# A 4 KB descriptor ring, five unread products on TensorE, and chunk 2's Am written by masked operations

## The chip, the core and the metric

The kernel runs on one core of a Trainium2 chip. The metric is the device time of one execution, in microseconds (us); three executions of the kernel before took 699.11, 699.98 and 702.73 us, so the median is 699.98 us. One more execution was recorded by the profiler and took 696.41 us; all rows below come from that one.

## What is computed

A linear recurrence over 768 steps for 4 x 8 heads of width 40, whose output of 3072 rows of 320 goes through a mixture of eight experts, one expert for each row.

```python
for t in range(S):                       # attention, per batch and head, state is 40 x 40
    y[t]  = r[t] @ state
    Sa    = state @ a[t]
    state = state * w[t] - outer(Sa, b[t]) + outer(v[t], k[t])
x = y.transpose(0, 2, 1, 3).reshape(3072, 320)
e = argmax(x @ w_gate, axis=1)           # one expert of 8 for each row
out = prob[e] * sigmoid(x @ w_output_gate)[e] * (relu(x @ w1[e]) @ w2[e])
```

## The kernel before

The 768 steps are cut into 12 chunks of 64. For each chunk c there are four kinds of work.

- `scan(c)` loads w and D (the a, k and b of the chunk, 1080 KB) and forms running products P and I of the decays on VectorE (DVE in the rows).
- `prep(c)` forms Av (a times decays; on VectorE for chunks 0 and 1, on GpSimd, POOL in the rows, from chunk 2 on) and KBt (k and b times decays, on VectorE), and spreads Av over a block matrix Am: of 120 partitions, three groups of 40 hold three groups of heads, and each head's columns are zero outside its own group. The product KBt x Am (tile `pl`, L213) then gives the chunk's coupling matrices, which ScalarE (ACT) copies into N and LA (L224, L226) and GpSimd masks (L228). Transposes (`back`, tile `pt`, L155) turn KBt into KB and Wp into WT.
- `tinv` inverts the triangular matrices of N on VectorE, alone for chunks 0 and 1 and in pairs after that; its result is copied to Tc by ScalarE (L319) for chunks 0 and 1.
- `crit(c, q)` and `tail(c, q)` carry the state through the chunk for each half q of the batches: products `pa` (L365, L378), with steps As on ScalarE (L369) and, for chunks 0 and 1, on VectorE (L391), then `pS`, `pM` and `pY`.

`run` interleaves these generators. The final order on each engine is made when the program is built, by a scheduler that places what it holds ready first; `issue_after` pins a block behind a given instruction of the same engine. Engines take their instructions in that order, each waiting for its semaphores, so an instruction that waits holds back all that stand behind it on its engine.

In `prep`, chunk 0 writes Am with three masked operations (one on ScalarE, two on VectorE, each with a mask `hj` over one group of partitions as scale). All later chunks fill only the non-zero blocks by three transfers on SyncE's queue (L184), and copy Av into LA by three more (`strips`, L170). `Am`, `KBt`, `Av`, `D`, `P` and `I` have one buffer each. Tiles `pl` and `pt` share two PSUM buffers. `warm` runs 40 unread products before the first input is there.

After the attention, `experts` gathers token rows with indirect transfers issued by GpSimd (L800), multiplies (L831, L844 to L846) and scatters rows (L849). GpSimd also scatters the routing table (`tab`, L712). GpSimd's transfers use descriptors kept in a ring in SBUF.

Of the kernel before, what the change touches and what calls it, by code (L numbers as in the profile page):

```python
# [9 lines left out]
F32 = mybir.dt.float32  # L10
F32R = mybir.dt.float32r
BF16 = mybir.dt.bfloat16
# [37 lines left out]
def pat(x, off, dims):  # L50

    return bass.AP(x.tensor, x.offset + off, [x.ap[0]] + [list(d) for d in dims])


class Att:
    npool = 0

    def __init__(s, ctx, tc, ident, stage, win, din, rl, vl, vt, nch=12):
        s.stage = stage
        s.tc, s.nc, s.nch, s.ident = tc, tc.nc, nch, ident  # L60
        s.win, s.din, s.rl, s.vl, s.vt = win, din, rl, vl, vt
        nc = s.nc
        pool = lambda n, b, **k: ctx.enter_context(tc.tile_pool(name=n, bufs=b, **k))
        s.p5, s.p2, s.cp = (pool(f"p{i}", i) for i in (5, 2, 1))
        s.ps = pool("ps", 1, space=PSUM)
        s.dr = pool("dr", 2, space=DRAM)
        s.pre = ExitStack()
        s.p1 = s.pre.enter_context(tc.tile_pool(name="p0", bufs=1))
        s.mM = s.cp.tile([128, C], F32, name="mM")
        nc.gpsimd.memset(s.mM, 1.0)  # L70
        for h in range(2):
            nc.gpsimd.affine_select(out=s.mM[64 * h:64 * h + 64], in_=s.mM[64 * h:64 * h + 64], pattern=[[1, C]],
                                    base=0, channel_multiplier=-1, compare_op=ALU.is_gt, fill=0.0)

        s.Am = s.p1.tile([120, 2, NP, 66], F32, name="Am")
        s.rst = s.p1.tile([120, 792], BF16, name="rst")
        with tc.high_priority():
            nc.vector.memset(s.rst, 0.0)
            nc.vector.memset(s.rst[:, 0:792:33], 1.0)
        s.Tt = s.p1.tile([128, 1056], F32, name="Tt")  # L80
        nc.gpsimd.memset(s.Tt, 0.0)
        nc.gpsimd.memset(s.Tt[:, 0:1056:33], 1.0)


        s.hj = s.cp.tile([120, 3], F32, name="hj")
        nc.vector.tensor_reduce(out=s.hj, in_=s.ident[0:120, 0:120].rearrange("p (j s) -> p j s", j=3), axis=AX.X, op=ALU.add)
        s.hm = s.cp.tile([128, 2], F32, name="hm")
        nc.vector.tensor_reduce(out=s.hm, in_=s.ident.rearrange("p (x h s) -> p h x s", x=4, h=2), axis=AX.XY, op=ALU.add)
        s.hq = s.cp.tile([128, 2], F32, name="hq")
        nc.vector.tensor_reduce(out=s.hq, in_=s.ident.rearrange("p (x h s) -> p h x s", x=2, h=2), axis=AX.XY, op=ALU.add)  # L90
        s.wb = s.cp.tile([120, 1], F32, name="wb")
        nc.gpsimd.memset(s.wb, -0.9)
        s.wsq = s.cp.tile([120, nch], F32, name="wsq")
        s.rqm = s.cp.tile([120, nch], F32, name="rqm")
        s.zb = s.cp.tile([128, 32], F32, name="zb")
        nc.gpsimd.memset(s.zb, 0.0)
        s.buffers()
        s.st, s.ld, s.post, s.idle, s.mark = {}, {}, [], False, {}
# [25 lines left out]
    def warm(s, src, n):  # L124
        fl = s.ps.tile([128, 512], F32, name="fl", tag="pS")
        for _ in range(n):
            s.nc.tensor.matmul(fl[0:32, 0:src.free_size()], s.zb[0:src.partition_size()], src, start=True, stop=True)

    def prep(s, c):

        nc = s.nc
        g, V = nc.gpsimd, nc.vector
# [18 lines left out]
        def back(dst, src):  # L151
            for g0, n, nj in ((0, 4, 3), (4, 2, 2)):
                pt = s.ps.tile([128, n, 40 * nj], F32, name="pt", tag="pl", bufs=2)
                for i in range(n):
                    nc.tensor.transpose(out=pt[:, i], in_=src[0:40 * nj, g0 + i].rearrange("p n t -> p (n t)"),  # L155
                                        identity=s.ident[0:40 * nj, 0:40 * nj])
                nc.scalar.copy(out=pat(dst, 40 * g0, [(240, nj), (40, n), (1, 40)]),
                                     in_=pt.rearrange("p g (j e) -> p j g e", j=nj))
                yield
# [7 lines left out]
        def strips():  # L167
            for j in range(3):
                ng = 6 if j < 2 else 4
                nc.sync.dma_start(out=LA[0:40, :, 6 * j:6 * j + ng, :], in_=Ag[40 * j:40 * j + 40, :, 0:ng])  # L170
# [7 lines left out]
        with s.tc.issue_after(s.mark['n', 0]) if c == 1 else ExitStack():  # L178
            nc.scalar.copy(out=Av[:, :, 64:66], in_=P[:, :, :, 32])
        Ag = Av.rearrange("p (a g) t -> p a g t", a=2)  # L180
        if c:
            for j in range(3):
                r, n = slice(40 * j, 40 * j + 40), 6 if j < 2 else 4
                am = nc.sync.dma_start(out=s.Am[r, :, 6 * j:6 * j + n], in_=Ag[r, :, 0:n]).ins  # L184
                s.mark['am', c] = am
            with s.tc.issue_after(am):
                strips()
        else:
            for j, (e, n) in enumerate(((nc.scalar, 6), (V, 6), (V, 4))):
                o, i, m = s.Am[:, :, 6 * j:6 * j + n, 0:64], Ag[:, :, 0:n, 0:64], s.hj[:, j:j + 1]  # L190
                if e is nc.scalar:
                    e.activation(out=o, in_=i, func=AF.Copy, scale=m)
                else:
                    e.tensor_scalar(out=o, in0=i, scalar1=m, scalar2=None, op0=ALU.mult)
            s.later = strips
        yield
        KBt = s.p1.tile([120, 12, 2, C], F32, name="KBt")
        with s.tc.issue_after(s.mark['r', 0]) if c == 1 else ExitStack():
# [7 lines left out]
        for side in range(2):  # L206
            Am = s.Am[:, side]
            yield
            for g0 in range(0, 6, 2):
                pl = s.ps.tile([128, 2, 3, C], F32, name="pl", tag="pl" if c or g0 == 0 else "tl", bufs=2 if c or g0 == 0 else 3)  # L210
                nj = 3 if g0 < 4 else 2
                for i in range(2):
                    nc.tensor.matmul(pl[:, i, 0:nj], KBt[:, 6 * side + g0 + i].rearrange("p n t -> p (n t)"), Am[:, g0 + i:g0 + i + 6 * nj - 5:6, 0:64],  # L213
                                     start=True, stop=True)
                pv = pl.rearrange("p g j t -> p j g t")
                for h in range(2):
                    r = slice(64 * side + 32 * h, 64 * side + 32 * h + 32)
                    n = C - 32 * h
# [12 lines left out]
        split()  # L231
        for side in range(2):
            yield from back(KB[:, side], KBt[:, 6 * side:6 * side + 6])
        yield from back(WT, Wp)
        yield

# [333 lines left out]
class Moe:  # L570
# [324 lines left out]
    def experts(s, ctx, verdict):  # L895
# [21 lines left out]
        def unit(e, t0, nt, prep):  # L917

            for _ in s.expert(nt, W[e], T[e, t0], lambda: s.hp, ps1, ps2) if (e, t0) != (0, 0) else s.E0:
                next(prep, None)  # L920
            for _ in prep:
                pass
# [197 lines left out]
```

## Time and profile before

| what | value |
|---|---|
| time, median of 3 (lowest to highest) | 699.98 us (699.11 to 702.73) |
| profiled execution, its own time | 696.41 us |
| its span, first to last instruction | 694.7 us |
| PE (TensorE) busy | 635.5 us, 91% |
| DVE (VectorE) busy | 463.8 us, 67% |
| ACT (ScalarE) busy | 338.2 us, 49% |
| POOL (GpSimd) busy | 229.7 us, 33% |
| mean granted clock of TensorE | 0.959 |

The span starts with the first instruction; 1.7 us of the execution lie around it. A busy PE is not a PE at its peak, and the granted clock stands at one of two levels, 1.00 or 0.50 of 2.4 GHz. In the rows, a time in brackets is how long the engine had been idle and, after the arrow, what ended that.

### The profile page before, as it was taken

The numbers are of one execution on the slowest core, as the hardware profiler recorded it, in microseconds if no ns is written. First come the engines' busy times: TensorE is split into PE (matmuls) and PEld (weight loads), VectorE is DVE, ScalarE is ACT, GpSimd is POOL, SyncE is SP. The second block draws the span as 40 slices with busy tenths as digits, with TensorE's granted clock in tenths as the row PEclk, the third lists the DMA queues.
The fourth block names the chain that finished last, engine by engine and source line by source line (L and its number), as shares of the span: only waits on it lengthen the run. The fifth ranks groups of instructions, "written<-read, shape, count | busy, mean of one in ns | idle before, by whom it ended". The sixth has DMA issues, their size and how long they took to land.

```text
span 694.7 us, 21145 instructions
## 1 busy us (share of the span) xinstructions
PE 635.5 (91%) x8866; PEld 568.2 (82%) x8866; DVE 463.8 (67%) x911; ACT 338.2 (49%) x782; POOL 229.7 (33%) x334
## 2 busy tenths in 40 slices
PE   7596987899999999999999899889999999999993
PEld 7375776788988888888898798789989989898993
DVE  8858689969987995998499544633774555444230
ACT  2576763774477367538733443432653444334110
POOL 9643321441343366224223102355241243311111
PEclk9657999999999999999999999999999999999997
DMA  5995662276356527633235822442673353510000
GB/s 139 174 187 135 173 154 69 86 175 163 103 144 162 126 84 192 162 95 103 63 81 171 232 69 71 137 124 74 202 218 110 102 176 113 170 58 23 28 11 22
DMA packets 56575, 84.79 MB, mean 122 GB/s; under 512 B 26878, under 2 KB 43785, under 8 KB 55033
## 3 DMA queue, kind: packets, MB, share of 16 engines
q1 hardware_dynamic: 52601, 74.39, 41.0%
q0 software_dynamic: 3872, 8.97, 4.5%
q8 instruction: 72, 1.18, 0.7%
q14 instruction: 30, 0.25, 0.1%
HBM read 67.59 MB, written 8.96 MB: 110 GB/s over the span
## 4 chain that ended last, share of the span: by engine, by line
PE 62%; DVE 18%; ACT 7%; issue 6%; DMA 5%; POOL 0%; POOLq 0%; SPq 0%; DVEq 0%; ACTq 0%
PE ph L831 12%; PE pa L378 6%; PE pM L450 5%; PE po L846 4%; PE po L844 4%; PE po L845 4%; PE pl L213 4%; PE pt L155 3%; PE pS L416 3%; DVE tmpf L300 3%; PE pY L466 3%; PE pa L365 3%; PE pY L465 3%; DMA out_dram<-y,ti 2%; PE pxt L636 2%
## 5 line engine op out<-in xcount | busy, mean ns | idle before, releaser
L836 DVE SCALAR_TENSOR_TENSOR hl<-ph,hh 128x480 fp32r<-128x480 f32 (+1 forms) x76 | 42.0, 563 | 62.1 <-ACT hh L835 61.4
L831 PE MATMUL ph<-xh,w1h 128*128 128x480 f32 (+1 forms) x228 | 80.1, 353 | 1.7 <-DVE hl L836 1.3
L849 POOL DMA_INDIRECT out_dram<-y,ti x32 | 34.4, 1076 | 139.9 <-DVE y L848 77.7
L844 PE MATMUL po<-w2h,hh 128*120 128x320 f32 x256 | 78.7, 313 | 0.9 <-ACT hh L835 0.9
L831 PE MATMUL ph<-xl,w1h 128*128 128x480 f32 (+1 forms) x228 | 78.6, 346 | 0.0
L835 ACT ACTIVATE hh<-ph 128x480 fp32r<-128x480 f32 (+1 forms) x76 | 37.0, 497 | 85.4 <-PE ph L831 77.3
L845 PE MATMUL po<-w2l,hh 128*120 128x320 f32 x256 | 77.8, 310 | 0.0
L846 PE MATMUL po<-w2h,hl 128*120 128x320 f32 x256 | 75.6, 311 | 0.2 <-DVE hl L836 0.2
L213 PE MATMUL pl<-Am,KBt 120*128 120x192 f32 (+1 forms) x288 | 64.1, 357 | 8.2 <-DMA Am<-Av 4.8
L228 POOL TENSOR_SCALAR_AFFINE_SELECT LA<-LA 64x192 f32<-64x192 f32 x144 | 52.9, 400 | 43.9 <-ACT LA L226 42.4
L224 ACT ACTIVATE N<-pl 32x192 f32<-32x192 f32 (+1 forms) x138 | 51.5, 373 | 30.5 <-PE pl L213 16.7
L369 ACT ACTIVATE As<-pa,hq 128x320 f32<-128x320 f32 x80 | 42.0, 528 | 47.5 <-PE pa L378 35.1
L213 PEld LDWEIGHTS pl<-Am,KBt 120*128 120x128 f32 x288 | 48.0, 209 | 14.1 <-issue 5.9
L712 POOL DMA_INDIRECT tab<-rec,si x24 | 30.8, 1284 | 86.4 <-DMA tab<-rec,si 38.8
L466 PE MATMUL pY<-KB,M 128*64 128x64 f32 (+1 forms) x768 | 53.4, 225 | 2.3 <-DVE M L454 2.3
L450 PE MATMUL pM<-R,VU 128*128 128x128 f32 x384 | 52.7, 288 | 1.5 <-ACT VU L442 1.4
L465 PE MATMUL pY<-Sd,R 128*64 128x64 f32 (+1 forms) x704 | 54.1, 227 | 0.0
L378 PE MATMUL pa<-As,Tc 64*32 64x40 f32 x1792 | 50.8, 204 | 2.1 <-ACT As L369 1.2
L831 PE MATMUL ph<-xh,w1l 128*128 128x480 f32 (+1 forms) x152 | 52.4, 345 | 0.0
L466 PEld LDWEIGHTS pY<-KB,M 128*64 128x64 f32 x768 | 47.0, 138 | 5.5 <-DVE M L454 2.4
L378 PEld LDWEIGHTS pa<-As,Tc 64*32 64x32 f32 x1792 | 40.0, 111 | 11.9 <-issue 3.5
L450 PEld LDWEIGHTS pM<-R,VU 128*128 128x128 f32 x384 | 46.9, 196 | 3.2 <-ACT VU L442 1.9
(194 smaller groups left out, 1554.2 us busy)
## 6 DMA issues: line engine op xcount, KB each, us to landing
D<-in_din_dram SPq DMA_DIRECT2D x12, 1080.0 KB
st<-in_w_dram SPq DMA_DIRECT2D x16, 512.0 KB
st<-in_w_dram SPq DMA_DIRECT2D x16, 480.0 KB
XS<-in_vt_dram SPq DMA_DIRECT2D x24, 256.0 KB
XU<-in_vt_dram SPq DMA_DIRECT2D x24, 256.0 KB
VU<-in_vl_dram SPq DMA_DIRECT2D x24, 208.0 KB
w<-in_win_dram SPq DMA_DIRECT2D x12, 371.2 KB
st<-in_w_dram SPq DMA_DIRECT2D x16, 256.0 KB
```

Source lines behind the costliest of these rows:

```text
L213: nc.tensor.matmul(pl[:, i, 0:nj], KBt[:, 6 * side + g0 + i].rearrange("p n t -> p (n t)"), Am[:, g0 + i:g0 + i + 6 * nj - 5:6, 0:64], sta ...
L224: s.mark['n', c] = nc.scalar.activation(out=nn, in_=pn, func=AF.Copy, scale=-1.0).ins
L228: g.affine_select(out=la[:, :, i], in_=la[:, :, i], pattern=[[0, nj], [1, C]], base=0, channel_multiplier=-1, compare_op=ALU.is_gt, fill=0.0)
L369: s.mark['as'] = nc.scalar.activation(out=x, in_=pa, func=AF.Copy, scale=s.hq[:, h:h + 1]).ins
L378: nc.tensor.matmul(pa[o + w:o + w + 32, i], m(p)[o:o + 64], x[o:o + 64, i, :], start=start, stop=True, tile_position=(o, o + w), skip_grou ...
L450: nc.tensor.matmul(pM[:, i], VU[:, h0 + i].rearrange("p n t -> p (n t)"), R[:, :, h0 + i], start=True, stop=True)
L465: nc.tensor.matmul(o, R[:, side, i, :], Sf[:, 40 * i:40 * i + w], start=True, stop=False)
L466: s.mark['y'] = nc.tensor.matmul(o, Ms[i // 4][:, i % 4, side, :], Kf[:, k:k + w], start=not c, stop=True).ins
L831: nc.tensor.matmul(ph, l, r, start=(i == 0), stop=(i == 7))
L844: nc.tensor.matmul(po, hh[f][:, ts_], w2h[:, f], start=(f == 0), stop=False)
L845: nc.tensor.matmul(po, hh[f][:, ts_], w2l[:, f], start=False, stop=False)
L846: nc.tensor.matmul(po, hl[f][:, ts_], w2h[:, f], start=False, stop=(f == 7))
```

## The change

There are three parts.

1. The ring of descriptors for GpSimd's transfers gets 4096 bytes of each partition in place of the default 16384.
2. `keep(5)`: once chunk 0's KB transposes are done, TensorE runs five products of a 120x32 bf16 tile of zeros `zh` with 512 columns of `rst` (bf16), into a PSUM tile that nobody reads. They stand behind the last of those transposes on TensorE.
3. Chunk 2's Am is written by masked operations as chunk 0's is: one on ScalarE (768 elements in each of 120 partitions), two on GpSimd (768 and 512). Its three transfers are gone. The LA strips remain transfers.

```diff
+        s.zh = s.p1.tile([120, 32], BF16, name="zh")
+        nc.gpsimd.memset(s.zh, 0.0)
...
+    def keep(s, n):
+        fl = s.ps.tile([32, 512], F32, name="fk", tag="pS")
+        with s.tc.issue_after(s.mark['pt']):
+            for _ in range(n):
+                s.nc.tensor.matmul(fl, s.zh, s.rst[:, 0:512], start=True, stop=True)
...
-                    nc.tensor.transpose(out=pt[:, i], in_=src[0:40 * nj, g0 + i].rearrange("p n t -> p (n t)"),
+                    s.mark['pt'] = nc.tensor.transpose(out=pt[:, i], in_=src[0:40 * nj, g0 + i].rearrange("p n t -> p (n t)"),
...
-        if c:
+        if c and c != 2:
...
             for j, (e, n) in enumerate(((nc.scalar, 6), (V, 6), (V, 4))):
+                e = e if c == 0 else nc.scalar if j == 0 else g
...
-            s.later = strips
+            if c == 0:
+                s.later = strips
+            else:
+                strips()
...
         for side in range(2):
             yield from back(KB[:, side], KBt[:, 6 * side:6 * side + 6])
+        if c == 0:
+            s.keep(5)
...
-    nc = _bacc.Bacc("TRN2", target_bir_lowering=False, num_devices=1)
+    nc = _bacc.Bacc("TRN2", target_bir_lowering=False, num_devices=1, dynamic_dma_scratch_size=4096)
```

The rows below are of the order in which instructions stand; line numbers of the changed kernel are up to 14 higher (L213 becomes L225, L228 becomes L240, L224 and L226 become L236 and L238).

GpSimd, chunk 2's Av and what follows, before:

```order
L177 TENSOR_TENSOR Av<-D,P 120x12x31
L228 AFFINE_SELECT LA<-LA 64x2x64 x2
L176 TENSOR_TENSOR Av<-D,I 120x12x33
L228 AFFINE_SELECT LA<-LA 64x3x64 x4
L228 AFFINE_SELECT LA<-LA 64x2x64 x2
```

and after:

```order
L185 TENSOR_TENSOR Av<-D,P 120x12x31
L240 AFFINE_SELECT LA<-LA 64x2x64 x2
L240 AFFINE_SELECT LA<-LA 64x3x64 x2
L184 TENSOR_TENSOR Av<-D,I 120x12x33
L203 TENSOR_SCALAR Am<-Av,hj 120x2x6x64
L203 TENSOR_SCALAR Am<-Av,hj 120x2x4x64
L240 AFFINE_SELECT LA<-LA 64x3x64 x2
L240 AFFINE_SELECT LA<-LA 64x2x64 x2
```

Two masks of chunk 1's LA now stand ahead of the second half of Av, and the two writes of Am between it and the other four masks.

ScalarE, the end of chunk 1's N and LA and the KB copies behind them, before:

```order
L226 ACTIVATE LA<-pl 64x2x2x64
L165 ACTIVATE Nm<-N,hm 128x16x16
L157 COPY KB<-pt 128x3x160
L157 COPY KB<-pt 128x2x80
L369 ACTIVATE As<-pa,hq 128x320
```

and after:

```order
L238 ACTIVATE LA<-pl 64x2x2x64
L201 ACTIVATE Am<-Av,hj 120x2x6x64
L173 ACTIVATE Nm<-N,hm 128x16x16
L165 COPY KB<-pt 128x3x160
L165 COPY KB<-pt 128x2x80
L383 ACTIVATE As<-pa,hq 128x320
```

One write of Am now stands ahead of Nm and the KB copies.

TensorE at chunk 0's KB transposes, after:

```order
L163 MATMUL pt<-ident,KBt 128x120 x4
L225 MATMUL pl<-Am,KBt 128x128 x2
L163 MATMUL pt<-ident,KBt 128x80 x2
L163 MATMUL pt<-ident,KBt 128x120 x4
L163 MATMUL pt<-ident,KBt 128x80 x2
L135 LDWEIGHTS zh
L135 MATMUL fk<-rst,zh 32x512
```

The last two rows come five times in turn, and the first `pa` of chunk 0 follows them; before, it followed the transposes directly. On TensorE and VectorE the order of chunk 1's and chunk 2's rows is otherwise as before up to about 80 us of the trace; from there to chunk 4 neighbouring rows change places, and so they do among the first experts' products (L831, L844 to L846, L808), where the transposes of the second set of gathered tokens (L808) stand five rows later than before. The rest of the program's order is the same.

## Rows read from the trace of the kernel before

**Rows 1.** Stretches of the span: busy us (instructions) by engine, granted clock, DMA share, GB/s
```profile
53.60:58.40 4.80, 0.08 (x5) 0.00 (x0) 4.66 (x10) 1.30 (x4) 0.00 (x0) 0.89 0.89 208
58.40:67.40 9.00, 8.46 (x83) 7.14 (x84) 8.11 (x17) 7.00 (x19) 5.09 (x10) 0.50 0.47 123
67.40:80.00 12.60, 12.34 (x170) 10.22 (x169) 7.34 (x12) 8.51 (x22) 1.95 (x6) 0.99 0.43 123
```

**Rows 2.** Timeline of PE: start, us, engine, line, operation, tiles, shapes, count, [idle before]
```profile
58.46 2.90 PE L213 MATMUL pl<-Am,KBt 120*128 120x192 f32 x8 [4.78 <-DMA Am<-Av]
...
62.49 1.22 PE L213 MATMUL pl<-Am,KBt 120*128 120x128 f32 x4
...
65.77 1.28 PE L378 MATMUL pa<-As,Tc 64*32 64x40 f32 x34
...
68.58 0.71 PE L213 MATMUL pl<-Am,KBt 120*128 120x128 f32 x4
```

**Rows 3.** Timeline of DVE, from chunk 1's inversion to its last step
```profile
51.27 0.49 DVE L254 SCALAR_TENSOR_TENSOR Ns<-tmpf,hm 128x256 f32<-128x256 f32 x1
...
53.75 0.95 DVE L200 TENSOR_TENSOR KBt<-D,I 120x768 f32<-120x768 f32 x1
...
55.80 1.80 DVE L114 TENSOR_TENSOR_SCAN I<-w,rst 120x792 f32<-120x792 f32 x1
...
62.54 0.06 DVE L106 MEMSET w<- 120x1 f32 x1 [0.76 <-ACT w L117]
62.62 0.99 DVE L391 TENSOR_TENSOR As<-As,pa 32x320 f32<-32x320 f32 x2
...
64.28 2.02 DVE L300 TENSOR_TENSOR tmpf<-Tt,Yt 128x256 f32<-128x256 f32 x2
...
66.85 1.12 DVE L316 STREAM_TRANSPOSE tmpf<-Tt 128x512 f32<-128x512 f32 x1
```

**Rows 4.** Timeline of ACT in the same stretch
```profile
53.95 0.52 ACT L204 COPY Wp<-P 120x372 f32<-120x372 f32 x1
...
61.45 0.94 ACT L117 ACTIVATE w<-w,wb 120x768 f32<-120x768 f32 x1
...
67.54 0.42 ACT L409 COPY XU<-pa 64x320 f32<-64x320 f32 x1
68.00 0.91 ACT L319 ACTIVATE Tc<-tmpf,hm 128x256 f32<-128x256 f32 x2
68.92 0.81 ACT L224 ACTIVATE N<-pl 32x384 f32<-32x384 f32 x2
```

**Rows 5.** Timeline of POOL: Av of chunk 2 and of chunk 3
```profile
47.58 0.96 POOL L176 TENSOR_TENSOR Av<-D,I 120x396 f32<-120x396 f32 x1
...
65.00 1.15 POOL L176 TENSOR_TENSOR Av<-D,I 120x396 f32<-120x396 f32 x1
```

**Rows 6.** Groups by line and shape: count | busy us, mean ns | idle before, releasers
```profile
L228 POOL TENSOR_SCALAR_AFFINE_SELECT LA<-LA 64x192 f32<-64x192 f32 x96 | 39.1, 437 | 38.7 <-ACT LA L226 37.7
L228 POOL TENSOR_SCALAR_AFFINE_SELECT LA<-LA 64x128 f32<-64x128 f32 x48 | 14.5, 326 | 5.2 <-ACT LA L226 4.7
L192 ACT ACTIVATE Am<-Av,hj 120x768 f32<-120x768 f32 x1 | 0.9, 942 | 0.1
```

**Rows 7.** Timeline of DVE in chunk 0's inversion
```profile
34.69 0.63 DVE L300 TENSOR_TENSOR tmpf<-Tt,Yt 128x256 f32<-128x256 f32 x2
```

**Rows 8.** Timeline of PE: after chunk 0's KB transposes, and a row at half clock
```profile
25.72 0.53 PE L155 MATMUL pt<-ident,KBt 80*128 80x80 f32 x2 [0.79 <-ACT KB L157]
30.09 0.45 PE L365 MATMUL pa<-XS,LA 64*64 64x64 f32 x2 [3.85 <-DMA XS<-in_vt_dram]
...
32.15 0.45 PE L365 MATMUL pa<-XS,LA 64*64 64x64 f32 x2 [0.62 <-DMA XS<-in_vt_dram]
...
443.59 0.41 PE L831 MATMUL ph<-xl,w1h 128*128 128x240 f32 x1
```

**Rows 9.** Timeline of PE among the first experts
```profile
457.35 0.28 PE L831 MATMUL ph<-xl,w1h 128*128 128x240 f32 x1
457.46 0.27 PE L831 MATMUL ph<-xh,w1l 128*128 128x240 f32 x1
460.20 0.63 PE L808 MATMUL px<-ident,xg 120*128 120x120 f32 x2 [2.46 <-DMA xg<-xd,ti]
```

**Rows 10.** Groups of POOL by line: GpSimd's scatters of the routing table
```profile
L712 POOL DMA_INDIRECT tab<-rec,si x24 | 30.8, 1284 | 86.4 <-DMA tab<-rec,si 38.8 <-DVE rec L709 30.8 <-DVE Tt L305 14.1
```

More of the change, by code (lines that the diff above doesn't have):

```diff
@@ L154, in back @@
                 for i in range(n):
-                    nc.tensor.transpose(out=pt[:, i], in_=src[0:40 * nj, g0 + i].rearrange("p n t -> p (n t)"),
-                                        identity=s.ident[0:40 * nj, 0:40 * nj])
+                    s.mark['pt'] = nc.tensor.transpose(out=pt[:, i], in_=src[0:40 * nj, g0 + i].rearrange("p n t -> p (n t)"),
+                                                       identity=s.ident[0:40 * nj, 0:40 * nj]).ins
                 nc.scalar.copy(out=pat(dst, 40 * g0, [(240, nj), (40, n), (1, 40)]),
```

## The prediction

> **What bounds the kernel now.** I read the page first: TensorE is busy for 91% of the span, so most of the run is a matter of TensorE's queue, and the change edits only the first tenth of it. I then cut the span into stretches. The one that the change aims at shows at once [rows 1]: from 53.6 to 58.4 us TensorE does next to nothing (0.08 of 4.80 us). The timeline of TensorE names what ended the hole: chunk 2's first product starts at 58.46 after 4.78 us of waiting for the transfers into Am [rows 2]. The chain of waits names the same transfers. So the stall is real, and it is the only long one that part 3 can remove.
>
> The next question is what else was under way during the hole, since an idle TensorE costs only what others then wait for. VectorE is busy in it for 4.66 of 4.80 us [rows 1]: it inverts chunk 1's matrices, writes chunk 2's KBt and runs chunk 3's scans, one after the other [rows 3]. Its last step of the inversion (L316) ends at 66.85 + 1.12 = 67.97 us. ScalarE copies that result at 68.00 us [rows 4], and since ScalarE takes its work in order, the rest of chunk 2's N and LA (68.92 us on) stands behind it. Just ahead of it, ScalarE's XU copies end at 67.96 us. Two chains therefore meet at 68.0 us with nothing to spare: the one through TensorE that holds the stall, and VectorE's inversion that does not. To move the program forward, both have to become shorter. In the stretch after that, TensorE is busy for 12.34 of 12.60 us at full clock [rows 1], and what is gained or lost at 68 us is handed on.
>
> **Part 3, chunk 2's Am, step by step.** It removes three transfers. Chunk 2's first product then needs Am and KBt. Av's second half ended at 47.58 + 0.96 = 48.54 us [rows 5]; two LA masks now stand ahead of it, 2 x 0.44 us [rows 6], so 49.4 us. No row shows GpSimd's masked multiplication. The nearest is the LA mask, also one tensor in and one out: 326 ns at 128 elements, 437 at 192 [rows 6], that is 1.73 ns an element and 0.10 us fixed. For 768 and 512 elements this gives 1.43 + 0.99 = 2.42 us; the two-input row (0.96 us for 396 elements, [rows 5]) gives 1280 x 2.42 ns = 3.1 us. I take 2.4, because it also has one input, and Am is whole at 51.8 us (52.5 at the other end). ScalarE's third lasts 0.94 us [rows 6]. KBt ends later, at 53.75 + 0.95 = 54.70 us [rows 3]. So the product starts at about 54.7 in place of 58.46: 3.76 us of the stall go, on TensorE's chain, and the next thing that is late there is KBt, not Am.
>
> On VectorE's chain two things change. First, the memset of w waited 0.76 us for ScalarE's square of w [rows 3]; that square stood behind chunk 2's first copies [rows 4], which now come 3.8 us earlier, so the wait goes: -0.76. Second, GpSimd works beside VectorE from 49.4 to 51.8 us. What that may cost shows at 64.28: two products that take 0.63 us elsewhere [rows 7] take 2.02 while GpSimd writes chunk 3's Av at 65.00 [rows 3, 5], a loss of 1.39. The first VectorE operation with two tensor inputs in the new overlap is L254 at 51.27 us; if it waits until GpSimd's write ends at 51.8, that is 0.56 later. Bounds: 0 (no collision) to 1.4 (one as bad as that at 64.28). I take +0.56, as the work that meets there is shorter than at 64.28. VectorE's chain thus ends 0.2 us earlier than before, and that, not 3.76, is what part 3 gives.
>
> The Trainium skill, page "GPSIMD Engine Reference", section "4.1 Engine selection", holds that one-input operations on GpSimd run at roughly line rate, against about twice as slow for two inputs. An estimate from that page's 1.2 GHz is 1280 / 1.2 = 1.07 us for both writes; L254 would then meet nothing and the sum below would be 0.56 us lower. The masks' rows, at 1.73 ns an element, speak against it, and no run here shows the multiplication itself.
>
> ScalarE's 0.94 us push Nm, the KB copies and the Wp copies later: Wp ends at 53.95 + 0.52 = 54.47 [rows 4], then 55.4 us. Chunk 3's scan, which overwrites what Wp reads, starts at 55.80 [rows 3]. The cover is 0.4 us, and nothing is left on the path; if it were gone, all 0.94 would fall on VectorE's chain. I cost it at nothing. The SyncE queue loses three entries; chunk 2's strips and chunk 3's D leave it no later. The DMA share of 0.89 in the hole [rows 1] falls, which can only help. Chunk 1's last four masks come some 3 us later on GpSimd; their reader is chunk 1's first `pa`, in the stretch after 67.4, so they are covered.
>
> **Part 2, the five products.** TensorE finishes chunk 0's KB transposes at 25.72 + 0.53 = 26.25 us and then waits 3.85 us for XS, until 30.09 [rows 8]. No row shows bf16 products of 512 columns. At half clock, as here, a 240-column product lasts 0.41 us [rows 8]; 512 columns then last 0.87, five of them 4.4 us, an upper bound, for neighbours overlap. They would end at 30.6 us at worst, 0.55 past the XS wait; TensorE waits for XS again for 0.62 us before 32.15 [rows 8], which covers that. Cost: 0, with +0.6 as the other end. A gain would need the clock to come back sooner. In this trace TensorE worked on after 58.46 with short gaps at clock 0.50 until 67.4 [rows 1]; five products with a wait behind them are less than that, so I expect no higher clock from them.
>
> **Part 1, the ring.** It changes no order, and no row of before shows GpSimd waiting for room in its ring. Where a scatter has to wait for an earlier transfer, the mean wait is 38.8 / 24 = 1.6 us [rows 10]. If three gathers ahead of the hole at 460.20 paid that, it would be 4.8 us on TensorE's path [rows 9]. I take 0 and keep the other end as a rival.
>
> **Moved rows.** In the stretch of chunks 2 to 4 neighbouring rows change places; I have no row that prices it and leave it in the range. Among the first experts, the transposes that wait 2.46 us for gathered tokens stand five products later; at 0.11 us from start to start [rows 9], -0.5 (bounds: -2.5, the whole wait, to +2.5, a wait as long again).
>
> **Sum.** -0.76 + 0.56 + 0 + 0 - 0.5 = -0.7 us. Against the profiled execution: 696.4 - 0.7 = 695.7. That execution is 3.6 us below the median of the runs; on the median the forecast is 699.98 - 0.7 = 699.3 us.
>
> **Rivals.**
> *The stall's worth passes through.* VectorE's inversion doesn't hold ScalarE, because its rows move up as far as TensorE's. Then 3.76 + 0.5 go, and the products of chunk 2 run at full clock: 0.71 for 1.22 us [rows 2], at least another 0.5. That gives 695.2. For it: the chain of waits runs straight through the Am transfers. Against it: 4.66 of 4.80 us busy on VectorE. Chance 0.28.
>
> *The clock stays low.* With its products done early, TensorE waits twice: for L391 (at 62.62, [rows 3]) and, after 65.77's products [rows 2], for ScalarE at 68.0 and the copies behind it. If the clock falls at the second wait, the full stretch after 68 [rows 1] starts at half clock. The same product takes 1.22 us at half and 0.71 at full clock [rows 2], so 42% of the time is lost; at half clock it stayed for 9.0 us in the trace [rows 1]: 0.42 x 9.0 = 3.8 us, so 703.1 us, slower than before, and about 704 if it returns later. It decides from the point where a hole of the size of that before 58.46 stands behind 66 us. The Trainium skill, page "TensorE: Matmul & The Clock Gate", section "HAM oscillation — how this bites in real kernels", states that a wait for data throttles TensorE and the next piece starts cold; the trace agrees, 0.89 in the hole and 0.50 after it. Chance 0.17.
>
> *The ring fills.* 699.3 + 4.8 = 704.1 us. For it: a quarter of the space. Against: GpSimd has idle time before most of its transfers. Chance 0.05.
>
> **How the numbers follow.** The forecast has 0.50. A measurement of this kernel can tell about 0.5% (3.5 us) from no change. Faster by more than that: the first rival, 0.28. Slower: half of the clock's 0.17, the ring's 0.05 and a rest of 0.04 for the moved rows, 0.17. Same: 0.55. The range takes in the first rival with 0.7 below it and the clock's case: 694.5 to 703.5 us.
>
> **What would show it.** In the profile after: chunk 2's first product starts near 54.7 us and waits for VectorE's KBt; GpSimd's two Am writes last 2.4 us together and L254 starts later beside them; ScalarE's Tc copy still waits for L316, near 67.8 us; the five products lie inside the XS wait. If Tc's copy comes at 65 us or before, the first rival holds. If the clock reads 0.50 after 70 us, the second does. A gap of over 1.5 us between GpSimd's gathers at 455 us would be the third.

## The result, and the profile after

The changed kernel takes 690.53 us (median of 5 executions, 689.39 to 695.56) against 699.43 us (median of 5, 697.9 to 702.73) for the kernel before: a ratio of 0.9887, 95% interval 0.9852 to 0.9922. It is 1.1% faster. The forecast of 699.3 us was wrong, and so was its range of 694.5 to 703.5 us.

| what | before | after |
|---|---|---|
| profiled execution, its own time | 696.41 us | 689.80 us |
| its span | 694.7 us | 688.0 us |
| TensorE (PE) busy | 635.5 us | 636.0 us |
| VectorE (DVE) busy | 463.8 us | 464.1 us |
| ScalarE (ACT) busy | 338.2 us | 339.7 us |
| GpSimd (POOL) busy | 229.7 us | 237.3 us |
| mean granted clock of TensorE | 0.959 | 0.966 |

Line numbers of the new kernel are higher, by up to 14: L225 is the old L213, L392 the old L378, L482 the old L468.

**The place that the change aims at.** First the stretches of after that answer to [rows 1], with the same columns (busy us and instructions by engine, granted clock, DMA share, GB/s).

```profile
53.60:58.40 4.80, 3.88 (x79) 3.19 (x78) 4.58 (x8) 3.31 (x8) 1.93 (x4) 1.00 0.92 210
58.40:67.40 9.00, 5.93 (x66) 4.88 (x66) 7.45 (x17) 7.61 (x20) 4.77 (x11) 0.62 0.31 81
67.40:80.00 12.60, 12.60 (x192) 10.56 (x191) 8.74 (x12) 8.54 (x22) 2.38 (x5) 1.00 0.59 157
```

TensorE's hole is gone: 3.88 us of work in the first stretch in place of 0.08. In the second it does 5.93 us in place of 8.46, because it now waits there, and VectorE is busy for 4.58 of 4.80 us as before. The timeline of TensorE in after (start, us, line, operation, tiles, shapes, count, idle time before and its end), for [rows 2, 8]:

```profile
26.39 2.31 PE L135 MATMUL fk<-rst,zh 120*32 120x512 bf16 x5
29.90 0.44 PE L379 MATMUL pa<-XS,LA 64*64 64x64 f32 x2 [1.20 <-DMA XS<-in_vt_dram]
...
53.80 0.76 PE L392 MATMUL pa<-As,Tc 64*32 64x40 f32 x32
54.50 1.57 PE L225 MATMUL pl<-Am,KBt 120*128 120x192 f32 x8
```

The first step of chunk 1's inversion on VectorE in before, which [rows 3] do not have:

```profile
49.76 1.09 DVE L252 STREAM_TRANSPOSE tmpf<-N 128x512 f32<-128x512 f32 x1
```

In after, that step and the rows that answer to [rows 3, 4]:

```profile
48.02 1.08 DVE L266 STREAM_TRANSPOSE tmpf<-N 128x512 f32<-128x512 f32 x1 [0.34 <-ACT N L236]
...
50.43 0.63 DVE L276 TENSOR_TENSOR tmpf<-Tt,Ns 128x8 f32<-128x8 f32 x1
...
52.49 1.10 DVE L212 TENSOR_TENSOR KBt<-D,I 120x768 f32<-120x768 f32 x1
...
61.07 0.06 DVE L108 MEMSET w<- 120x1 f32 x1
...
64.89 1.10 DVE L330 STREAM_TRANSPOSE tmpf<-Tt 128x512 f32<-128x512 f32 x1
```

```profile
66.03 0.91 ACT L333 ACTIVATE Tc<-tmpf,hm 128x256 f32<-128x256 f32 x2 [0.80 <-DVE tmpf L330]
```

And for GpSimd, for [rows 5]:

```profile
44.84 0.91 POOL L185 TENSOR_TENSOR Av<-D,P 120x372 f32<-120x372 f32 x1 [0.99 <-DMA XS<-in_vt_dram]
...
47.07 0.97 POOL L184 TENSOR_TENSOR Av<-D,I 120x396 f32<-120x396 f32 x1
48.15 3.77 POOL L203 TENSOR_SCALAR Am<-Av,hj 120x768 f32<-120x768 f32 x2
```

Chunk 2's first product starts at 54.50 us, 3.96 us earlier, with no wait for Am. It doesn't wait for KBt either, which is whole at 52.49 + 1.10 = 53.59 us: TensorE is still at the products before it. The last step of VectorE's inversion (L330, L316 before) starts at 64.89, only 1.96 us earlier, and ScalarE, which had nothing to spare for it before, now waits 0.80 us for it. Of the 1.96 us, 1.74 were there when the inversion began (48.02 in place of 49.76), before GpSimd's and ScalarE's writes of Am.

**The whole span.** The saving can be followed by two landmarks: the last output of the attention, and GpSimd's last scatter. In before (one row of VectorE's, one of GpSimd's timeline):

```profile
436.90 0.49 DVE L468 TENSOR_TENSOR x<-pY,WT 128x320 f32<-128x320 f32 x1 [1.64 <-PE pY L466]
```

```profile
685.50 1.00 POOL L849 DMA_INDIRECT out_dram<-y,ti  x1 [3.53 <-DVEq L1092]
```

In after:

```profile
436.25 0.49 DVE L482 TENSOR_TENSOR x<-pY,WT 128x320 f32<-128x320 f32 x1 [1.63 <-PE pY L480]
```

```profile
683.08 1.00 POOL L863 DMA_INDIRECT out_dram<-y,ti  x1 [2.58 <-DMA out_dram<-y,ti]
```

Of the 6.7 us between the spans, 436.90 - 436.25 = 0.65 us are gained up to the end of the attention, 248.60 - 246.83 = 1.77 us from there to the last scatter, and (694.7 - 685.50) - (688.0 - 683.08) = 9.20 - 4.92 = 4.28 us behind the last scatter, where the kernel computes nothing any more. The instructions of that last place have one line, and one of them differs: GpSimd's DRAIN (count, then shortest/median/longest in ns, then first and last start). Before:

```profile
L1116 POOLq DRAIN  x3: 46/112/7511, 686.3 to 694.4; - x3
```

After:

```profile
L1130 POOLq DRAIN  x3: 46/113/3212, 683.9 to 687.7; - x3
```

The longest DRAIN stands behind the last scatter, and the last instructions of all other engines come after its end. It lasts 7.51 us before and 3.21 us after: 4.30 us, all of the 4.28. The prediction never looked at this row. This is one pair of executions; the experiments show which of the three pieces stand.

### The profile page after: what moved, and what is told of

Its sections match the earlier page's. It is cut to its first block, busy times and chain, and to the rows that moved or that the text cites. A ratio compares the mean times of both kernels' runs of the same rounds, so it can differ in the third digit from the quotient of the medians.

```text
span 688.0 us, 21149 instructions
## 1 busy us (share of the span) xinstructions
PE 636.0 (92%) x8871; PEld 567.0 (82%) x8871; DVE 464.1 (67%) x911; ACT 339.7 (49%) x783; POOL 237.3 (34%) x337
## 3 DMA queue, kind: packets, MB, share of 16 engines
q8 instruction: 72, 1.18, 0.7%
## 4 chain that ended last, share of the span: by engine, by line
PE 55%; DVE 24%; ACT 8%; DMA 7%; issue 5%; SPq 1%; POOLq 0%; POOL 0%; ACTq 0%; DVEq 0%
PE ph L845 12%; PE pa L392 5%; PE po L860 4%; PE pM L464 4%; PE po L858 4%; PE po L859 4%; DVE tmpf L314 4%; PE pl L225 4%; PE pt L163 3%; ACT N L236 3%; DVE I L116 2%; PE pS L430 2%; DVE P L116 2%; DMA out_dram<-y,ti 2%; DMA st<-in_w_dram 2%
## 5 line engine op out<-in xcount | busy, mean ns | idle before, releaser
L240 POOL TENSOR_SCALAR_AFFINE_SELECT LA<-LA 64x192 f32<-64x192 f32 x144 | 54.7, 413 | 42.2 <-ACT LA L238 40.8
L225 PE MATMUL pl<-Am,KBt 120*128 120x192 f32 (+1 forms) x288 | 60.9, 343 | 7.5 <-ACT LA L238 7.0
L236 ACT ACTIVATE N<-pl 32x192 f32<-32x192 f32 (+1 forms) x138 | 51.5, 374 | 25.8 <-PE pa L392 12.2
L726 POOL DMA_INDIRECT tab<-rec,si x24 | 29.0, 1209 | 89.8 <-DMA tab<-rec,si 37.2
L225 PEld LDWEIGHTS pl<-Am,KBt 120*128 120x128 f32 x288 | 45.3, 199 | 13.3 <-ACT LA L238 9.6
L392 PE MATMUL pa<-As,Tc 64*32 64x40 f32 x1792 | 51.1, 204 | 2.3 <-ACT As L383 1.7
L814 POOL DMA_INDIRECT xg<-xd,ti x32 | 38.7, 1210 | 33.7 <-PE px L822 16.7
L392 PEld LDWEIGHTS pa<-As,Tc 64*32 64x32 f32 x1792 | 40.2, 112 | 12.1 <-issue 3.5
```

What stands on the lines that cost most here:

```text
L236: s.mark['n', c] = nc.scalar.activation(out=nn, in_=pn, func=AF.Copy, scale=-1.0).ins
L240: g.affine_select(out=la[:, :, i], in_=la[:, :, i], pattern=[[0, nj], [1, C]], base=0, channel_multiplier=-1, compare_op=ALU.is_gt, fill=0.0)
L392: nc.tensor.matmul(pa[o + w:o + w + 32, i], m(p)[o:o + 64], x[o:o + 64, i, :], start=start, stop=True, tile_position=(o, o + w), skip_grou ...
```

## The experiments

**Theories.** D: the last DRAIN grows with the ring, and part 1 gives most of the gain. C, its rival: the end differs because five more instructions on TensorE shift where the end's code lies. K: the five products pay by bringing the clock back earlier. O: the rows that the scheduler moves pay. P: the Am stall's 3.8 us pass through. Differences in us below are the ratio less one, times 699.4. The recorded ratios are not those of the medians: a difference of medians can lie up to 1.8 us off (the whole change, repeated: 691.96 against 699.06 us, -7.1 us in place of -8.9).

**Each part alone.** The ring on the kernel before:

```diff
-    nc = _bacc.Bacc("TRN2", target_bir_lowering=False, num_devices=1)
+    nc = _bacc.Bacc("TRN2", target_bir_lowering=False, num_devices=1, dynamic_dma_scratch_size=4096)
```

> Part 1 alone: the ring of 4 KB on the kernel before, with no other edit; the order of instructions is that of before on every engine. Theory D (the drain): the largest single piece of the gain is GpSimd's last DRAIN, which lasted 7.5 us after the last scatter in before and 3.2 us after the change, because it grows with the ring. Then the first 680 us look like before, the last DRAIN is about 3.2 us, and the time is 4.3 us below before (about 695.1 against 699.4, ratio 0.994). Theory C (place of the code): the end differs because the five products shift where the instructions of the end lie, and the ring does nothing; then the DRAIN stays at 7.5 us and the time at 699.4 (ratio 1.000). My recorded step costed the ring at 0, with +4.8 as its other end.

Ratio 0.9954 (0.9927 to 0.998), -3.2 us. Its DRAINs:

```profile
L1116 POOLq DRAIN  x3: 46/113/3044, 692.1 to 695.7; - x3
```

The order of before and a DRAIN of 3.04 us: D holds, C falls. From the start of the last scatter to the end of the span it takes 9.20 to 9.21 us in all five executions recorded with 16 KB and 4.7 to 5.0 us in all seven with 4 KB. Chunk 2's Am alone, which is part 3 and nothing else:

```diff
-        if c:
+        if c and c != 2:
...
+                e = e if c == 0 else nc.scalar if j == 0 else g
...
-            s.later = strips
+            if c == 0:
+                s.later = strips
+            else:
+                strips()
```

> Part 3 alone: chunk 2's Am by masked operations, no five products, ring as before. Theory S (hidden stall, as recorded): chunk 2's first product starts near 54.5 in place of 58.46 us, but the clock is still half until 50 us and VectorE's inversion for chunk 1 still ends near 67.5 us, so the end moves by -0.7 to 0 (ratio 0.999 to 1.000). Rival P (the stall passes through): L316 of chunk 1 starts at 64.9 or before and the time is 4 us below before (ratio 0.994). On both the last DRAIN is 7.5 us if theory D holds, and anything else if it is a matter of code places.

Ratio 0.9982 (0.9952 to 1.0012), -1.3 us. GpSimd's writes are apart here, so each shape has its duration (timeline of GpSimd):

```profile
48.71 1.58 POOL L195 TENSOR_SCALAR Am<-Av,hj 120x512 f32<-120x512 f32 x1
...
51.13 2.21 POOL L195 TENSOR_SCALAR Am<-Av,hj 120x768 f32<-120x768 f32 x1
```

The first product starts at 54.15 us and the inversion's last step (L316 in the lines of before) at 65.04. Here the product does wait for KBt:

```profile
54.15 1.54 PE L217 MATMUL pl<-Am,KBt 120*128 120x192 f32 x8 [0.37 <-DVE KBt L204]
```

L316 comes near P's 64.9, but the kernel with the ring alone, which has before's order there, starts L316 at 65.67; 1.18 us of the 1.81 are no work of Am. The interval leaves out P's -4. The five products alone, with `zh`, `keep` and the mark as in part 2:

```diff
+        if c == 0:
+            s.keep(5)
```

> Part 2 alone: the five products, with the other order of the chunks 2 to 4 and of the first experts that comes with them, ring as before. Theory K (clock): the granted clock rises near 40 us in place of 50.5, chunk 1's inversion starts near 48.0 in place of 49.76 us; the transfers into Am still end near 58, so of these 1.7 us half or more is lost there again; among the experts the wait for gathered tokens falls from 2.5 to about 1.2 us. Together -1 to -3 us (ratio 0.996 to 0.9985). Rival (as recorded: the five products give no higher clock): the clock rises at 50 us and the time is within 0.5 us of before. Last DRAIN: 7.5 us by theory D, 3.2 us by theory C, since the five products are here.

Ratio 1.0125 (1.0086 to 1.0165): 8.7 us slower, which neither side expected. Without Am, the scheduler answers the five products with a third order, and in chunks 2 to 4 TensorE waits more. Waits of TensorE from 80 to 130 us (what for, us in total, times, longest), and the stretch as a whole:

```profile
PE pS L426 <- DVE tmS L434: 4.3, 1, 4.3
PE pa L388 <- ACT As L379: 1.7, 3, 0.9
```

```profile
80.00:130.00 50.00, 35.94 (x731) 30.62 (x730) 42.98 (x85) 22.34 (x57) 10.95 (x18) 0.93 0.41 103
```

TensorE does 35.94 us of work here against 41.37 in before (below). So an order of rows can be a large term. DRAIN: 7.51 us, against C once more.

**The parts together, and the ring's size.** Parts 2 and 3 with the ring of 16 KB, that is the whole change less this:

```diff
-    nc = _bacc.Bacc("TRN2", target_bir_lowering=False, num_devices=1, dynamic_dma_scratch_size=4096)
+    nc = _bacc.Bacc("TRN2", target_bir_lowering=False, num_devices=1)
```

> Parts 2 and 3 without the ring of 4 KB; the order is that of the changed kernel on every engine. Theory D: everything as in the changed kernel up to the last scatter (about -2.4 us there), and a last DRAIN of 7.5 us: about 4.3 us above the changed kernel, so some -4.6 us against before (ratio 0.993 to 0.996). Theory C: DRAIN 3.2 us and the time of the changed kernel (ratio 0.989).

Ratio 0.9969 (0.9945 to 0.9994), -2.2 us, and

```profile
L1130 POOLq DRAIN  x3: 46/113/7500, 682.7 to 690.7; - x3
```

The same kernel again, on another chip:

> Parts 2 and 3 with the ring of 16 KB once more, now on the same chip as the next three. Additive theory: 4.4 us above the whole change for the DRAIN alone, so 2 to 3 us below before (ratio 0.996 to 0.997), with a DRAIN of 7.5 us. Rival G2 (the small ring costs something among the experts): in the profiles so far the stretch from attention's last step (the last L468 in the lines of before) to the last scatter took 246 to 249 us with 16 KB and 247 to 251 us with 4 or 2 KB. If that is the ring's doing, this kernel keeps 246 to 247 us there and is only 2 to 3 us above the whole change, as the first pair of runs had it (-2.9 against -7.1).

Ratio 0.9922 (0.9891 to 0.9954), -5.5 us; the DRAIN is 7.50 us. From the last output of the attention to the last scatter it took 251.0 us (434.45 to 685.46), more than in any of the seven executions with 4 KB (246.8 to 250.6): the stretch varies between 246 and 251 us with either ring, and G2 falls. This one kernel was measured at -2.2 us and at -5.5, so a difference between two such measurements can be off by 3 us. The whole change, repeated:

> The changed kernel once more, beside the next three on one chip. Additive theory: the ring takes 4.4 us off GpSimd's last DRAIN (7.5 to 3.1 us), Am and the five products with their order another 2 to 3, so 692.0 to 693.0 against 699.2 (ratio 0.990 to 0.991). Rival: the first measured difference (ratio 0.9887) is all real and something comes only from the three parts together; then ratio 0.987 to 0.989.

Ratio 0.9873 (0.9833 to 0.9913), -8.9 us: the result stands, and the interval holds both the additive 0.990 and its rival. Its profiled execution has a span of 694.3 us though, against 688.0 for the same kernel above, with the DRAIN at 3.13 us. A pair of traces can differ by 6 us with no change in the code. The whole change with 8 KB, and with 2048 in the same place:

```diff
-    nc = _bacc.Bacc("TRN2", target_bir_lowering=False, num_devices=1, dynamic_dma_scratch_size=4096)
+    nc = _bacc.Bacc("TRN2", target_bir_lowering=False, num_devices=1, dynamic_dma_scratch_size=8192)
```

> The whole change with a ring of 8 KB. DRAINs so far: 7.50 us at 16 KB, 3.04 to 3.21 at 4 KB, 2.49 at 2 KB. A straight line through 4 and 16 KB gives 4.6 us here, and the time 1.5 us above the whole change (ratio 0.990 to 0.992). Rival F (a floor of some 3 us up to a size, then the ring's length): 3.1 us. By rival G2 the stretch among the experts is shorter than with 4 KB, and the time is that of the whole change or 1 us below.

> The whole change with a ring of 2 KB in place of 4. If the last DRAIN goes linearly with the ring (7.5 us at 16 KB, 3.1 at 4 KB: 0.37 us a KB and 1.6 us fixed), it is 2.4 us here and the time 0.7 us below the whole change. Rival F (a floor): the DRAIN also waits for the last scatter, whose transfers land 2.4 to 2.7 us after its start, so it stays at 2.5 to 3.1 us and the time is the same. Rival G (the ring is too small for the gathers): GpSimd's gathers wait for room, at 455 us and after, and the time rises by 3 us or more.

8 KB: ratio 0.9909 (0.988 to 0.9939). 2 KB: 0.9903 (0.9873 to 0.9933). Neither can be told from 4 KB. The DRAINs, of 8 KB and of 2 KB:

```profile
L1130 POOLq DRAIN  x3: 46/113/3609, 685.6 to 689.8; - x3
```

```profile
L1130 POOLq DRAIN  x3: 46/112/2486, 685.5 to 688.6; - x3
```

So: 7.49 to 7.51 us in five executions with 16 KB, 3.61 with 8 KB, 3.02 to 3.30 in seven executions with 4 KB, 2.49 with 2 KB. It falls with the ring, but at 8 KB both expected forms missed (4.6 by the straight line, 3.1 by the floor); at 2 KB 2.49 lies next to either (2.4, and 2.5 to 3.1). What DRAIN does in that time isn't visible in a trace. One hint: with 16 KB it ends 4.7 to 5.1 us after SyncE is through with its waits at the end, with 8 KB 1.06, with 4 KB 0.49 in each of the seven executions, with 2 KB 0.03. So the shortest ones seem to end with what SyncE waits for there, and a floor near 2.5 us stays possible; neither is shown. By G the smallest ring should have lost 3 us among the gathers, and it did not.

**The products and the moved rows.** Ring and Am without products, in the order of before; against the whole change (this kernel also has no `zh`, no memset of it and no `keep`):

```diff
-        if c == 0:
-            s.keep(5)
```

> Ring of 4 KB and chunk 2's Am, without the five products; the order of TensorE, VectorE and the rest is that of before, but for Am's own entries. Additive theory: -4.4 for the ring and -1.3 for Am: 693.5 (ratio 0.992). If the five products and the order that comes with them are worth something, this kernel is 1 to 2 us above the whole change of the same call; if they are worth nothing, the two lie within 1 us. My recorded steps (-0.2 for Am, 0 for the ring, 0 for the products) would give 699.0.

Ratio 0.9916 (0.9882 to 0.995), -5.9 us. With three products the order stays that of before; with four (`s.keep(4)` in the same place) it becomes that of the changed kernel, on every engine:

```diff
-            s.keep(5)
+            s.keep(3)
```

> Three products in place of five, with ring and Am: with three the order stays that of before, with four and more it becomes that of the changed kernel. So this run has the products (1.4 us of TensorE in place of 2.3) without the moved rows. Theory K (the products pay by the clock): it comes below the kernel without products by 1 to 2 us, and in its trace the clock rises at 40 to 46 us. Theory O (the moved rows pay): it equals the kernel without products, and the whole change is lower than both. Theory N (neither pays): all three within 1 us.

Ratio 0.9932 (0.9904 to 0.9961), -4.8 us: not below the kernel without products. Then both on one chip:

> Three products and the order of before, ring and Am as in the whole change, beside four on one chip. Theory O: 2 to 3 us above four, at -4.5 us against before as in its first run. Theory N: within 1 us of four.

> Four products in place of five, ring and Am as in the whole change. With four the order is that of the changed kernel, with three (next run) that of before: one product and the moved rows lie between the two. Theory O (the moved rows pay): equal to the whole change, -7 to -8 us against before (ratio 0.989), and 2 to 3 us below three. Theory N: equal to three, -4.5 to -6 us.

Three: 0.9932 (0.9909 to 0.9956), -4.8 us. Four: 0.9878 (0.9851 to 0.9906), -8.5 us. The intervals don't meet; one more product, 0.43 us of TensorE inside a wait, can't be 3.7 us by its own time. So what comes with the fourth product pays, and that is the other order: O, though by which way is less clear (below). Three other pairs, each on one chip and with intervals that overlap: five against three gives -4.1 us (-8.9 against -4.8), five against none -3.0 with ring and Am (-8.9 against -5.9) and only -0.9 with Am and 16 KB (-2.2 against -1.3). The stretch in which most rows moved, in before, in three and in four:

```profile
80.00:130.00 50.00, 41.37 (x945) 35.41 (x945) 43.12 (x86) 27.15 (x69) 15.49 (x28) 1.00 0.48 117
```

```profile
80.00:130.00 50.00, 41.28 (x891) 35.77 (x890) 41.82 (x85) 25.04 (x64) 14.95 (x26) 0.93 0.46 111
```

```profile
80.00:130.00 50.00, 43.14 (x943) 36.90 (x937) 43.45 (x88) 27.90 (x71) 14.61 (x30) 1.00 0.47 115
```

TensorE gets through 43.14 us of work in place of 41.28. In all seven executions recorded in the new order it is 43.1 to 43.6 us, in the six recorded in before's 41.2 to 42.4. The waits of TensorE there tell which went. In three:

```profile
PE pY L480 <- DVE M L468: 2.3, 1, 2.3
PE pxt L646 <- DVE x L482: 1.3, 1, 1.3
PE pS L430 <- DVE tmS L438: 1.0, 1, 1.0
PE pl L225 <- ACT Wp L216: 0.8, 1, 0.8
```

In four:

```profile
PE pY L480 <- DVE M L468: 3.0, 3, 1.2
PE pa L392 <- ACT As L383: 1.0, 2, 0.7
```

The waits for x, for tmS of L438 and for Wp are gone from the list, the longest fell from 2.3 to 1.2 us, and the whole lists come to 8.5 and 6.6 us. That is 1.9 us in this stretch. Most of it isn't kept: from the attention's first output x to its sixth, near 180 us, it takes 96.7 to 98.2 us in the three executions of before's order whose clock stays at 1.00 in the stretch, and 96.0 to 98.4 in the seven of the new order (medians 97.7 and 97.4).

A second piece is the clock: in the other three executions in before's order it fell to 0.50 for some 7 us between 110 and 129 us (0.93 on average in the row of three), in none of the seven in the new order. From the first output to the last (VectorE's rows of x: line, count, shortest/median/longest in ns, first and last start), in three and in four:

```profile
L482 DVE TENSOR_TENSOR x<-pY,WT x24: 475/488/492, 83.0 to 444.1; 128x320 f32<-128x320 f32 x24
```

```profile
L482 DVE TENSOR_TENSOR x<-pY,WT x24: 472/484/492, 81.2 to 436.7; 128x320 f32<-128x320 f32 x24
```

It takes 357.0 to 361.1 us in the three executions with that fall, 353.3 to 356.2 in the three of before's order without it and 353.1 to 356.3 in the seven of the new order. So the rows' own waits explain little, and most of what the traces show goes with the clock. That the order keeps the clock up is likely, but three executions against none don't show it. Whether the rows moved among the first experts pay too stays open.

The clock's return after 40 us is theory K's subject. One stretch in the two executions recorded of the changed kernel, first the one shown above, then the repeated one (the clock is the third number from the end):

```profile
41.00:43.40 2.40, 2.08 (x40) 1.66 (x39) 0.73 (x1) 2.32 (x7) 2.35 (x4) 1.00 0.96 170
```

```profile
41.00:43.40 2.40, 2.40 (x36) 1.92 (x35) 0.76 (x1) 2.31 (x8) 2.35 (x4) 0.50 0.98 174
```

One kernel, two clocks: it rose at 39.9 us in one execution and at 45.5 in the other. Without products it rose at 43.7, 45.0, 45.6 and 50.5 us, with three at 45.4 and 50.5, with four or five between 39.9 and 45.5. Chunk 1's inversion starts at 49.7 and 49.8 us in the two executions with a rise at 50.5 (before is one of them) and at 47.9 to 48.8 in all twelve others. So four or five may bring the clock earlier, but a rise at 40 bought nothing there over one at 45; three against none is no gain, and products of that number without the moved rows could not be tried, since the scheduler moves the rows as soon as the fourth is there.

## Why the prediction was wrong, step by step

- **Part 1 is the step that failed first: "I take 0".** It measures -3.2 us alone (from -5.1 to -1.4), and the traces show 4.2 to 4.5 us behind the last scatter. The prediction priced the ring by waits between transfers [rows 10] and saw only a loss as its other end. It never asked what else on GpSimd handles the ring, and never read the 9.2 us between the last scatter and the end of the span, though the chain of waits ends at that scatter, at 686.5 us of 694.7. The third rival ("the ring fills") did not occur: 0.31 us lie between GpSimd's gathers after 455 us, in after as in before.
- **Moved rows, "-0.5", was mis-sized.** The row that priced the move among the first experts, 2.46 us of waiting [rows 9], says little: the wait for gathered tokens was 1.2 us in one execution of the changed kernel and 4.5, at the set of tokens before, in the other. The order as a whole is worth -3.7 us by four against three, and -0.9 to -4.1 by the other pairs; another order, that of the products alone, cost 8.7. The prediction left the stretch of chunks 2 to 4 "in the range" with no price, though TensorE's waits there, which are in before those of the kernel with three, were at hand: 8.5 us in all, as an upper bound. The new order took 1.9 of them and kept less, and the rest of its worth goes with the clock as far as the traces tell. How the order pays stays open in part.
- **Part 3 was right in mechanism and nearly in size.** The first product was forecast at 54.7, waiting for KBt, and came at 54.50. That is partly luck: KBt was whole 1.1 us earlier, at 53.59, and TensorE's own products stood ahead; the forecast wait for KBt is there in the kernel with Am alone (0.37 us). GpSimd's writes were put at 2.42 us and took 3.77, 2.9 ns an element: more even than the two-input bound of 3.1 us. The Trainium skill, page "GPSIMD Engine Reference", section "4.1 Engine selection", gives one-input operations roughly line rate; the estimate of 1.07 us from that page's clock is 3.5 times too low here, and the measurement decides. The longer writes cost nothing, since GpSimd came to Av 1.13 us earlier (44.84 us, 45.97 in before): the writes began at 48.15 in place of the forecast's 49.4 and ended at 51.92 (forecast 51.8), so the size and the start were both off and made up for each other. VectorE's wait of 0.76 us before the memset is gone (the memset starts at 61.07 us with no wait). The collision came, on L276's 128x8 product and not on L254: 0.63 us where the same operation takes 0.17 in before, 0.46 lost against 0.56 forecast. Which operation is hit differs between executions; from the inversion's first step to the end of KBt VectorE takes 4.94 us in before and 4.95 with the ring alone, 5.57 in after and 5.66 with Am alone, so 0.6 to 0.7 are lost. L316 gained 1.96 us in the traces, not 0.2, but from the inversion's first step to L316 it is 17.09 us in before and 16.87 in after: 0.22, the forecast's size. The other 1.74 came ahead of it, where the clock was back at 39.9 us and not at 50.5. ScalarE waits 0.80 us for the inversion: VectorE's chain, not the stall, does hold the program, as the prediction said. Part 3 measures -1.3 us (from -3.4 to +0.8), against -0.2.
- **Part 2.** Five products took 2.31 us, not up to 4.4, and lay inside the wait for XS, of which 1.20 us are left. "I expect no higher clock from them" is not settled: it came back earlier in some executions, and three products gained no time.
- **The first rival** ("the stall's worth passes through", 695.2) fell: Tc's copy comes at 66.03 us, between its 65 and the forecast's 67.8, and Am alone isn't worth 4 us. **The second** ("the clock stays low") did not occur: the clock did fall behind a second wait (0.62 on average from 58.4 to 67.4 us), but it reads 1.00 from 67.4 to 80 us.
- **The sum** with the measured terms: ring -3.2, Am -1.3, order -3.7: -8.2 us, against a measured -7.9. That they agree so well is luck: Am's interval runs from -3.4 to +0.8, and the order's term from -0.9 to -4.1 with the pair that one takes. It was the range that should have held this. Its low end took in the stall's rival and left out a gain by the ring, for which no row stood, and by the order, for which there were some.

## What to carry to other kernels

Follow the chain past the last useful instruction: what lies between it and the end of the span is time like any other, and a setting that touches no instruction can change it. Where an edit makes a scheduler build another order, the order is a term of its own: price it by the waits in the stretch where the rows move, separate it from the edit by the smallest edit that flips it, and follow a landmark past the stretch to see how much of the gain is kept. And ask of a landmark that moved by a microsecond or two whether it also moves between executions of one kernel.

## What was not expected of the hardware

GpSimd's DRAIN behind the last indirect transfer lasted 7.5 us with a descriptor ring of 16 KB a partition, 3.6 with 8 KB, 3.0 to 3.3 with 4 KB and 2.5 with 2 KB, and in all 14 executions the last instructions of every other engine came after it. TensorE's clock came back at 39.9 us in one execution of a kernel and at 45.5 in another, and the spans of these two were 688.0 and 694.3 us; 3.8 of the 6.3 us lie among the experts, so the clock's return is not shown to be the cause.
